# Rows of wo in one transfer per group, and loads of M's forms and stores of M at other places of a linear-attention kernel

## The chip, the cores and the metric

The kernel runs on one core of a Trainium2 chip. The time is the device time of one execution in microseconds; where several runs were made, their median. The profile is one further execution, recorded by the hardware profiler. Its span goes from the first to the last instruction.

## What is computed

Two linear-attention blocks, A and B, with the same shapes (x is 2048 x 640, 32 heads of 20), side by side in the output:

```python
qkv = (x @ wqkv).reshape(B, S, 3, H, Dh)             # q, k, v; H = 32, Dh = 20
phi = lambda t: jnp.where(t > 0, t + 1, jnp.exp(t)) + 1e-6
pq, pk = phi(q), phi(k)
kv = jnp.einsum("bhsd,bhse->bhde", pk, v)
z = jnp.einsum("bhsd->bhd", pk)
num = jnp.einsum("bhqd,bhde->bhqe", pq, kv)
den = jnp.einsum("bhqd,bhd->bhq", pq, z)[..., None] + 1e-6
return (num / den).transpose(...).reshape(B, S, D) @ wo     # of A and of B, concatenated
```

## The kernel before

**What it works on.** The values v are never formed. A Gram matrix G = phi(k)^T x is summed over the 2048 rows, each head's kv is G times its columns of wv, and M = kv times the rows of wo of that head: a 640 x 640 matrix per block. The output is then phi(q), divided by the denominators, times M. Products of fp32 values are split into a high and a low half (names ending in h and l) and made of three matmuls.

**Two phases.** In the first half (the k phase, to about 282 us) a planner orders the work. `note(engine, cost, function, writes, reads, ahead, dma, ...)` records a job with its cost and the transfer that it starts; the planner sorts the jobs of each engine by costs and due times. G of A and of B, and kv and M of A (`kvmm`, `mmm` L648), are made here. M of A goes to memory by SP (`md<-mev`, L670), and is read back (`m<-md`, L369) and turned into ten "forms" (sums and differences of blocks of M, split in two halves), which `m_forms` (L705) stores to memory (L713).

In the second half (the q phase) the order is written by hand: `at(slot, f, ...)` puts a call behind a slot, and the slots are `("q", u, c, k)`, unit u of 512 rows, chunk c of 5, step k of 5, and `("o", u, s)`. Units 0 to 3 are A's, 4 to 7 B's. `qmm` (L1144) makes q of a chunk: three matmuls per step (L1015 to L1017; in the first chunk of units 0 and 1, L1153, L1154 and, for the product with the low half of x, L1159 after the others). It needs x in two halves: `xqs`, loaded from the input and rounded by ScalarE (`load_xraw`, L1046), and `xql`, loaded from a copy that the k phase left in memory (`load_xq`, L1050). `psd` (L1193) are the denominators, `outmm` (L1289, matmuls L1313) the product with the forms. For A these are loaded by `form_load` (L1140: tiles `fh`, `fl`, `fm`, from `fdh`, `fdl`).

M of block B is made during unit 0 of the q phase: `load_o` loads the rows of wo, `kvmm2` makes kv, `mmm2` (called three times, i = 0 to 2, matmuls `psm` at L615) makes M of groups 2i and 2i + 1, and `store_m` stores it from GpSimd (L1082).

**The rows of wo.** The heads lie in six groups: four of 6 heads (120 rows of wo), two of 4 (80 rows). A tile of 128 partitions takes a group's first 64 rows in its lower half and the last 64 in its upper half; the halves share 8 or 48 rows, which the kv tile masks. `load_wo` (L628) loads it in two transfers of 64 rows on SP's queue, 160 KB each. In the k phase the planner calls it for A, two groups before each of three `mmm` (L653); in the q phase the slot ("q", 0, 0, 0) calls it for all six groups of B.

**Stores of M.** `m_rows` (L617) gives the rows of M of half a group: in memory 20 blocks of 3 (or 2) rows that lie 32 rows apart, in the tile 60 (or 40) partitions.

**Queues.** SP issues loads in its program order. Its transfers use eight semaphores in turn, so each is issued only when the one eight before it has landed.

Of the kernel before, what the change touches and what calls it, by code (L numbers as in the profile page):

```python
# [15 lines left out]
DH = 20  # L16
# [61 lines left out]
class Plan:  # L78
# [9 lines left out]
    def note(self, engine, n, fn, w, r, ahead=None, dma=None, late=None, by=None, due=None, safe=0.0, lat=0.0):  # L88
        base = self.RATE.get(engine)
        j = Job(engine, base[0] + base[1] * n if base else n, fn, ahead, dma)  # L90
        for part, writes in [(p, True) for p in w] + [(p, False) for p in r]:
            sp = part.space
            if sp.where is not None and sp not in j.spaces:
                j.spaces.append(sp)
            for lo, hi, other, wrote in sp.uses:
                if lo < part.hi and part.lo < hi and (writes or wrote) and other is not j:
                    j.deps.add(other)
            if writes:
                sp.uses = [u for u in sp.uses if not (part.lo <= u[0] and u[1] <= part.hi and u[2] is not j)]
            sp.uses.append((part.lo, part.hi, j, writes))  # L100
        for d in j.deps:
            d.nexts.append(j)
        for sp in j.spaces:
            sp.left += 1
        if engine == "PE":
            j.ideal = self.pe_at
            self.pe_at += j.cost
        j.late = self.pe_at + (25.0 if late is None else late)
        if by is not None:
            j.late = self.pe_at + by  # L110
        j.by, j.set, j.safe, j.lat = by, due, safe, (LAT if due is None else 1.9) + lat
        self.jobs.append(j)
        return j
# [105 lines left out]
def tile_linear_attn_pair(ctx: ExitStack, tc: tile.TileContext, ins, out: bass.AP):  # L219
    nc = tc.nc  # L220
    P = 128
    S, D = ins[0]["x"].shape
# [58 lines left out]
    note = plan.note  # L281
# [329 lines left out]
    def m_products(o, i, wo, hs):  # L611

        for p in (0, 64):
            for j in range(2):
                nc.tensor.matmul(o[p // 64][j * 64:j * 64 + 64, :HF],  # L615
                                 kvt[p:p + 64, 2 * i + j], wo[j][p:p + 64, hs], start=True, stop=True)

    def m_rows(b, i, a):

        rows = md[b].rearrange("(d h) n -> d h n", h=H)  # L620
        out = []
        for j in range(2):
            h0, nh = GROUPS[2 * i + j]
            n = nh // 2
            out.append((rows[:, h0 + a * n:h0 + a * n + n, :], slice(j * 64, j * 64 + DH * n)))
        return out

    def load_wo(eng, to, b, g):  # L628
        h0, nh = GROUPS[g]
        for p, row in ((0, h0 * DH), (64, (h0 + nh) * DH - 64)):  # L630
            eng.dma_start(to[p:p + 64], ins[b]["wo"][row:row + 64, :])

    def kvmm(k):
        ws = []
# [13 lines left out]
    def mmm(i):  # L648
        n = gn[0] - (3 if i % 2 else 4)
        ks = ((3, 4, 5)[n % 3], (3, 4, 5)[(n + 1) % 3], 6, 7)  # L650
        wo, m = ([Space(n, D, ANY) for _ in range(2)] for n in ("wo", "mev"))
        for j in range(2):
            note("SP", 0.14, lambda j=j: load_wo(nc.sync, wo[j].all.f, 0, 2 * i + j), [wo[j].all], [], ahead=14.0, dma=1.0)  # L653

        def products():
            for h in range(2):
                o = [BK[k].open("psm") for k in ks[2 * h:2 * h + 2]]
                m_products(o, i, [x.all.f for x in wo], slice(h * HF, h * HF + HF))

        note("PE", 1.3, products, [BK[k].all for k in ks], [x.all for x in wo] + [KVT.all])  # L660
        for h in range(2):
            hs = slice(h * HF, h * HF + HF)
            for a in range(2):
                k = ks[2 * h + a]
                note("ACT", HF, lambda a=a, k=k, hs=hs: act(m[a].all.f[:, hs], BK[k].tile[:, :HF], AF.Copy), [m[a][hs]],
                     [BK[k].all])
        for a in range(2):
            for j, (rows, part) in enumerate(m_rows(0, i, a)):
                w = 4 * i + 2 * a + j
                note("SP", 0.07, lambda a=a, rows=rows, part=part: nc.sync.dma_start(rows, m[a].all.f[part]),  # L670
                     [mdv[w:w + 1]], [m[a].all], dma=0.5)
# [87 lines left out]
    a, z, x = jh[0][0:P], jl[0][0:P], jr[0][0:P]  # L759
# [127 lines left out]
    for p in range(4, NPB):  # L887
        i, h = divmod(p - 2, 2)
# [9 lines left out]
    for p in range(NPB + 1, NP):  # L898
        if p == NPB + 1:
            fl = kvs  # L900
        else:
            i, h = divmod(p - NPB - 2, 2)
            gready(NG + i)
            fl = filled(NG + i, h, p in (NPB + 2, NP - 1))
        for (q, n), i in place.items():
            if q == p - NPB:
                fl.setdefault(n, []).append((mmm, i))
        kpair(p, fl)
        if p == NPB + 4:
            zsums(0)  # L910
        if p == NPB + 5:
            m_forms()
# [8 lines left out]
    j = note("HOST", 0.0, swap, [gate.all], [])  # L921
# [50 lines left out]
    for g, (h0, nh) in enumerate(GROUPS):  # L972
        cols = NC * DH * nh
        w = Space("wv", cols, (BD,))
# [46 lines left out]
    def at(slot, f, *a):  # L1021
        todo.setdefault(slot, []).append((f, a))
# [34 lines left out]
    def load_o(b, g):  # L1057
        tag = ("dsh0", "dsl0", "dsh1", "dsl1", "dah1", "dal1")[g]
        o = q2[0].tile([P, D], F32, name="wo", tag=tag, bufs=1)
        load_wo(nc.sync, o, b, g)  # L1060
        wot[b, g] = o
# [309 lines left out]
            at(a, form_split, b, i)  # L1371
            at(s, form_store, b, i)

    for i in range(6):
        at((("q", 0, 2, 1), ("q", 0, 2, 4), ("q", 0, 3, 1), ("q", 1, 0, 0), ("q", 1, 0, 2), ("q", 1, 1, 0))[i],
           form_load, 0, i)
    for i in range(6, 10):
        at(("q", 1, i - 5, 4) if i < 9 else ("q", 1, 4, 0), form_load, 0, i)

    for g in range(NGR):  # L1380
        at(("q", 0, 0, 0), load_o, 1, g)
# [1 line left out]
    for i in range(3):  # L1383
        at((("q", 0, 3, 1), ("q", 0, 4, 0), ("q", 0, 4, 4))[i], mmm2, 1, i)
        for h in range(2):
            at((("q", 0, 3, 3), ("q", 0, 3, 4), ("q", 0, 4, 2), ("q", 0, 4, 3), ("q", 1, 0, 1), ("q", 1, 0, 3))[2 * i + h],
               store_m, nc.gpsimd)

    for c, a in ((0, ("q", 1, 4, 1)), (2, ("q", 1, 4, 1)), (4, ("q", 2, 0, 3)), (1, ("q", 4, 0, 2)), (3, ("q", 4, 0, 2))):
# [11 lines left out]
    h = NG - 1  # L1401
# [26 lines left out]
    for v in range(1, NU):  # L1428
        w, u = v - 1, v + 1
# [8 lines left out]
        else:  # L1438
            a = (5, 6, 7, 8, 8, 10, 11) if v == 1 else (2, 3, 5, 6, 7, 9, 11)
# [75 lines left out]
```

## Time and profile before

| | |
|---|---|
| median of 3 runs | 567.69 us (566.89 to 568.5) |
| the profiled execution | 569.47 us |
| its span | 567.7 us, granted TensorE clock 0.994 |
| busy: PE, DVE, ACT, POOL | 557.9, 414.3, 351.5, 74.6 us |
| moved by the DMA engines | 119.60 MB, mean 211 GB/s |
| wo of A, wo of B | 12 and 12 transfers of 160 KB, 6.7 and 5.2 us to landing |

PE is TensorE's matmuls, PEld its weight loads, which overlap them; DVE is VectorE, ACT ScalarE, POOL GpSimd, SP the engine that only issues transfers. A row of the timeline has the start, the length, engine, line, operation and tiles, and in brackets the idle time ahead of it and what ended that. "SPq" and "POOL DMA_DIRECT2D" rows are issues of transfers: their length is that of the issuing, not of the transfer. "PEclk" is the granted clock as a share of the full one; the DMA share is the mean busy share of the core's 16 DMA engines (the packets' times add up to a little over 1 when all are full).

### The profile page before, as it was taken

What the parts mean: (1) busy time and instruction counts of PE and PEld (TensorE: products, weight loads), DVE (VectorE), ACT (ScalarE), POOL (GpSimd) and SP (SyncE); (2) the same over time, 40 slices, a digit from 0 to 9 for tenths busy, and PEclk for the clock granted to TensorE, in tenths of its full rate; (3) what the DMA queues carried; (4) which work ended last, traced back from release to release, by engine and by line L of the source; (5) the groups of instructions that cost most, each with busy time, mean ns of one, the idle gap of its engine ahead of it and who ended that gap; (6) DMA issues with size and microseconds to landing.
All of it is one profiled execution on the core that took longest, in us unless ns stands there. A gap on an engine that the chain in (4) does not pass through costs nothing.

```text
span 567.7 us, 9238 instructions
## 1 busy us (share of the span) xinstructions
PE 557.9 (98%) x3368; PEld 501.2 (88%) x3368; DVE 414.3 (73%) x657; ACT 351.5 (62%) x644; POOL 74.6 (13%) x127
## 2 busy tenths in 40 slices
PE   8999999999999999999999799999999999999997
PEld 6999999989998899998885589898989989898997
DVE  7788687589987668887632499967788686767792
ACT  6777475574768647676227268775767666665551
POOL 1210111111113001111215003110012201001010
PEclk9999999999999999999999799999999999999999
DMA  8994765849869577897999965763363997122022
GB/s 313 377 259 117 184 166 114 270 110 312 257 136 268 185 191 225 240 273 212 353 282 326 373 236 164 272 218 120 107 241 124 346 389 262 48 75 92 1 94 92
DMA packets 69509, 119.60 MB, mean 211 GB/s; under 512 B 7320, under 2 KB 30776, under 8 KB 69464
## 3 DMA queue, kind: packets, MB, share of 16 engines
q1 hardware_dynamic: 59576, 90.39, 48.0%
q0 software_dynamic: 9600, 28.23, 18.0%
q8 instruction: 26, 0.43, 0.3%
q10 hardware_dynamic: 288, 0.39, 0.3%
q14 instruction: 19, 0.16, 0.1%
HBM read 72.44 MB, written 36.07 MB: 191 GB/s over the span
## 4 chain that ended last, share of the span: by engine, by line
PE 93%; DMA 4%; DVE 2%; issue 0%; ACT 0%; SPq 0%; DVEq 0%; ACTq 0%
PE psg L547 19%; PE pa L1313 12%; PE ka L315 10%; PE psq L1015 7%; PE psq L1016 7%; PE psq L1017 7%; PE pe L1313 6%; PE ke L315 5%; PE psr L547 5%; PE psk L812 4%; PE psb L1313 4%; PE kb L315 3%; DMA xql<-xd 2%; PE pskv L602 1%; DMA xqs<-in_A_xt 1%; PE psm L615 1%
## 5 line engine op out<-in xcount | busy, mean ns | idle before, releaser
L1015 PE MATMUL psq<-xqh,wh 128*128 128x512 f32 x190 | 74.8, 394 | 0.0
L1017 PE MATMUL psq<-xqh,wl 128*128 128x512 f32 x190 | 74.6, 393 | 0.0
L1016 PE MATMUL psq<-xql,wh 128*128 128x512 f32 x190 | 74.5, 392 | 0.0
L547 PE MATMUL psg<-pkh,xnl 128*128 128x512 f32 x160 | 63.0, 394 | 0.0
L547 PE MATMUL psg<-pkl,xnh 128*128 128x512 f32 x160 | 63.0, 393 | 0.0
L547 PE MATMUL psg<-pkh,xnh 128*128 128x512 f32 x160 | 62.4, 390 | 0.0
L1173 DVE SCALAR_TENSOR_TENSOR pq<-eq,rq 128x512 f32<-128x512 f32 x40 | 27.6, 691 | 44.2 <-ACT rq L1172 44.2
L1171 ACT ACTIVATE eq<-psq 128x512 f32<-128x512 f32 x40 | 24.0, 600 | 55.3 <-PE psq L1017 44.7
L493 ACT ACTIVATE kt<-ka 128x320 f32<-128x320 f32 x52 | 22.6, 435 | 56.3 <-PE ka L315 56.1
L410 POOL DMA_DIRECT2D zacc<-ek x32 | 26.2, 819 | 198.2 <-DVE ek L503 164.8
L1328 ACT ACTIVATE o<-pa 128x320 f32<-128x320 f32 x64 | 27.9, 438 | 26.2 <-PE pa L1313 25.5
L1015 PEld LDWEIGHTS psq<-xqh,wh 128*128 128x128 f32 x190 | 36.0, 189 | 8.3 <-issue 1.0
L1017 PEld LDWEIGHTS psq<-xqh,wl 128*128 128x128 f32 x190 | 36.0, 189 | 7.7
L1016 PEld LDWEIGHTS psq<-xql,wh 128*128 128x128 f32 x190 | 36.0, 189 | 7.3
L547 PEld LDWEIGHTS psg<-pkh,xnl 128*128 128x128 f32 x160 | 30.0, 188 | 6.5
L547 PEld LDWEIGHTS psg<-pkh,xnh 128*128 128x128 f32 x160 | 30.1, 188 | 4.9
L547 PEld LDWEIGHTS psg<-pkl,xnh 128*128 128x128 f32 x160 | 30.0, 188 | 4.8
L503 DVE SCALAR_TENSOR_TENSOR ek<-ek,kt 128x640 f32<-128x640 f32 x26 | 21.4, 821 | 16.2 <-ACT kt L502 16.2
L405 ACT ACTIVATE pkh<-ek,epst 128x640 fp32r<-128x640 f32 x32 | 26.4, 827 | 5.7 <-DVE ek L503 5.7
L406 DVE SCALAR_TENSOR_TENSOR pkl<-ek,pkh 128x640 fp32r<-128x640 f32 x32 | 26.2, 820 | 3.7 <-ACT pkh L405 3.7
L560 DVE TENSOR_TENSOR gacc<-psg,gacc 128x512 f32<-128x512 f32 x30 | 20.5, 688 | 11.6 <-PE psg L547 11.3
L309 DVE TENSOR_TENSOR xnl<-xns,xnh 128x640 fp32r<-128x640 f32 x32 | 25.6, 819 | 0.8 <-ACT xnh L306 0.8
(225 smaller groups left out, 1638.4 us busy)
## 6 DMA issues: line engine op xcount, KB each, us to landing
zacc<-ek POOLq DMA_DIRECT2D x32, 320.0 KB, 4.6
xql<-xd SPq DMA_DIRECT2D x40, 256.0 KB, 5.7
xd<-xl SPq DMA_DIRECT2D x29, 320.0 KB, 4.0
out<-o POOLq DMA_DIRECT2D x28, 320.0 KB, 3.9
xns<-in_A_x SPq DMA_DIRECT2D x16, 320.0 KB, 4.6
xts<-in_B_xt_tiles SPq DMA_DIRECT2D x16, 320.0 KB, 4.4
xns<-in_B_x SPq DMA_DIRECT2D x16, 320.0 KB, 5.8
xqs<-in_A_xt SPq DMA_DIRECT2D x20, 256.0 KB, 6.2
```

What stands on the lines that cost most here:

```text
L309: note("DVE", n, lambda: tt(lo.r, src.f, hi.f, op=OP.subtract), [lo], [src, hi], ahead=10.0)
L315: nc.tensor.matmul(o, a.r, w.r, start=start and k == i == 0, stop=k == n - 1 and i == 2, skip_group_check=True)
L405: note("ACT", n + 110, lambda: act(hi.r, p.f, AF.Identity, bias=epst), [hi], [p, K0.all], by=8.0)
L406: note("DVE", n, lambda: stt(lo.r, p.f, EPS, hi.f, op0=OP.add, op1=OP.subtract), [lo], [p, hi], by=9.0)
L410: note("POOL", 1.0, lambda: nc.gpsimd.dma_start(z.f, p.f, **kw), [z], [p], dma=1.0 if first else 1.86)
L547: nc.tensor.matmul(o[:, :n], a.r, w.r, start=j == 0 and q == 0, stop=j == 2 and q == 2, skip_group_check=True)
L1015: nc.tensor.matmul(o, whi, xhi, start=first, stop=False)
L1016: nc.tensor.matmul(o, whi, xlo, start=False, stop=False)
L1017: nc.tensor.matmul(o, wlo, xhi, start=False, stop=last)
L1173: nc.vector.scalar_tensor_tensor(pq[u][:, c, :], e, 1.0, r, op0=OP.min, op1=OP.add)
L1313: nc.tensor.matmul(ps, x, y, start=start and n == i == 0, stop=n == len(terms) - 1 and i == 2, skip_group_check=True)
L1328: copy = lambda x, y: nc.scalar.activation(x, y, AF.Copy)
```

## The change

Three edits. `load_wo` makes one transfer of 128 rows in place of two of 64: the source is an access pattern of two runs of 64 rows that overlap, the second starting (20 nh - 64) rows after the first; the planner's cost of a call is halved. The loads of A's forms are called from other slots, with form 8 ahead of 6 and 7. The stores of B's M are called from later slots.

```diff
     def load_wo(eng, to, b, g):
         h0, nh = GROUPS[g]
-        for p, row in ((0, h0 * DH), (64, (h0 + nh) * DH - 64)):
-            eng.dma_start(to[p:p + 64], ins[b]["wo"][row:row + 64, :])
+        w = ins[b]["wo"][h0 * DH:(h0 + nh) * DH, :]
+        eng.dma_start(to, bass.AP(w.tensor, w.offset, [[(nh * DH - 64) * D, 2], [D, 64], [1, D]]))
...
-            note("SP", 0.14, lambda j=j: load_wo(nc.sync, wo[j].all.f, 0, 2 * i + j), [wo[j].all], [], ahead=14.0, dma=1.0)
+            note("SP", 0.07, lambda j=j: load_wo(nc.sync, wo[j].all.f, 0, 2 * i + j), [wo[j].all], [], ahead=14.0, dma=1.0)
...
-    for i in range(6):
-        at((("q", 0, 2, 1), ("q", 0, 2, 4), ("q", 0, 3, 1), ("q", 1, 0, 0), ("q", 1, 0, 2), ("q", 1, 1, 0))[i],
-           form_load, 0, i)
...
+    for i, a in ((0, ("q", 0, 1, 0)), (1, ("q", 0, 1, 3)), (2, ("q", 1, 0, 1)), (3, ("q", 1, 0, 4)), (4, ("q", 1, 1, 1)),
...
-            at((("q", 0, 3, 3), ("q", 0, 3, 4), ("q", 0, 4, 2), ("q", 0, 4, 3), ("q", 1, 0, 1), ("q", 1, 0, 3))[2 * i + h],
+            at((("q", 0, 4, 2), ("q", 0, 4, 3), ("q", 1, 0, 3), ("q", 1, 0, 4), ("q", 1, 1, 2), ("q", 1, 1, 3))[2 * i + h],
                store_m, nc.gpsimd)
```

The orders of TensorE, VectorE, ScalarE and GpSimd are the same in both programs, the stores of M on GpSimd included. SP's differs. This is SP at the start of the q phase in the kernel before (fdh_100 and fdl_101 are the halves of form 0, 102 and 103 of form 1, and so on; xd_87 is the copy of x of unit 1):

```order
L302 DMA wv<-in_B_wv 128x400 x2
L631 DMA wo<-in_B_wo 64x640 x12
L1046 DMA xqs<-in_A_xt 128x512
L1140 DMA fh<-fdh_100 128x640
L1140 DMA fl<-fdl_101 128x640
L1046 DMA xqs<-in_A_xt 128x512 x4
L1140 DMA fh<-fdh_102 128x640
L1140 DMA fl<-fdl_103 128x640
L1140 DMA fh<-fdh_104 128x640
L1140 DMA fl<-fdl_105 128x640
L1050 DMA xql<-xd_87 128x512 x5
```

And the same place of SP's order after the change:

```order
L302 DMA wv<-in_B_wv 128x400 x2
L631 DMA wo<-in_B_wo 128x1x640 x6
L1046 DMA xqs<-in_A_xt 128x512
L1140 DMA fh<-fdh_100 128x640
L1140 DMA fl<-fdl_101 128x640
L1140 DMA fh<-fdh_102 128x640
L1140 DMA fl<-fdl_103 128x640
L1046 DMA xqs<-in_A_xt 128x512 x4
L1050 DMA xql<-xd_87 128x512 x5
L1140 DMA fh<-fdh_104 128x640
L1140 DMA fl<-fdl_105 128x640
```

Twelve transfers of wo became six of 128 rows; form 1 moved ahead of four of the xqs, and form 2 behind the five xql of unit 1. In the k phase only the loads of wo differ; this is SP around the second of the three pairs of groups of A (xd_91 is the copy of x of unit 5, md_98 is M of A):

```order
 L349 DMA xd_91<-xl 640x1x128
 L302 DMA xts<-in_B_xt_tiles 128x640 x2
-L631 DMA wo<-in_A_wo 64x640 x4
+L631 DMA wo<-in_A_wo 128x1x640 x2
 L349 DMA xd_91<-xl 640x1x128 x2
 L670 DMA md_98<-mev 20x3x640 x4
```

Four transfers became two at the same place, ahead of the stores of x and of M.

More of the change, by code (lines that the diff above doesn't have):

```diff
@@ L1372, in forms2 @@
             at(s, form_store, b, i)
-    for i in range(6):
-        at((("q", 0, 2, 1), ("q", 0, 2, 4), ("q", 0, 3, 1), ("q", 1, 0, 0), ("q", 1, 0, 2), ("q", 1, 1, 0))[i],
-           form_load, 0, i)
-    for i in range(6, 10):
-        at(("q", 1, i - 5, 4) if i < 9 else ("q", 1, 4, 0), form_load, 0, i)
+    for i, a in ((0, ("q", 0, 1, 0)), (1, ("q", 0, 1, 3)), (2, ("q", 1, 0, 1)), (3, ("q", 1, 0, 4)), (4, ("q", 1, 1, 1)),
+                 (5, ("q", 1, 1, 4)), (8, ("q", 1, 2, 1)), (6, ("q", 1, 2, 4)), (7, ("q", 1, 3, 1)), (9, ("q", 1, 4, 0))):
+        at(a, form_load, 0, i)
     for g in range(NGR):
```

## The prediction

> **What bounds the kernel now.** I read the page first, then the waits of TensorE, then the chain, then the timeline round the one hole that the waits name.
>
> ```profile
> span 567.7 us, 9238 instructions
> PE 557.9 (98%) x3368; PEld 501.2 (88%) x3368; DVE 414.3 (73%) x657; ACT 351.5 (62%) x644; POOL 74.6 (13%) x127
> PE psq L1159 <- DMA xql<-xd: 4.4, 3, 3.5
> ```
>
> The first two lines are the page's, the third is from the waits of PE between 282 and 330 us (total, times, longest). TensorE is busy 98% of the span, and the one wait of a microsecond or more there is for the transfer xql. The chain (start, length, what) and TensorE's timeline show the place.
>
> ```profile
> 300.51 6.17 DMA xqs<-in_A_xt
> 306.75 10.28 DMA xql<-xd
> 317.07 1.93 PE psq L1159 x3
> ```
>
> ```profile
> 299.12 1.31 PE L615 MATMUL psm<-wo,kv 64*64 64x320 f32 x16
> 303.30 1.31 PE L615 MATMUL psm<-wo,kv 64*64 64x320 f32 x16
> 307.48 1.31 PE L615 MATMUL psm<-wo,kv 64*64 64x320 f32 x16
> ...
> 310.89 0.39 PE L1154 MATMUL psq<-xqh,wl 128*128 128x512 f32 x1
> 314.76 0.63 PE L1159 MATMUL psq<-xql,wh 128*128 128x512 f32 x1 [3.48 <-DMA xql<-xd]
> ...
> 321.79 0.41 PE L1194 MATMUL psd<-ac,same 128*128 128x512 f32 x1
> 322.04 0.40 PE L1015 MATMUL psq<-xqh,wh 128*128 128x512 f32 x1
> ```
>
> Three products M of block B (psm) run at 299.12, 303.30 and 307.48 without waiting. Then unit 1 runs dry at 311.1 and waits until xql has landed. From 310.89 to 322.04 only 14 matmuls start; at the step of 0.23 us of the others there (311.12 minus 310.89) they take 3.2 us, so the hole costs 11.15 - 3.2 = 7.9 us. Part of that is the clock, in the windows (span, then busy time of five engines, granted clock, DMA share, GB/s):
>
> ```profile
> 136.00:212.00 76.00, 76.00 (x570) 68.58 (x569) 57.26 (x103) 49.17 (x91) 12.85 (x18) 1.00 0.76 215
> 290.00:300.00 10.00, 9.73 (x156) 7.90 (x155) 2.98 (x6) 2.10 (x5) 2.19 (x4) 1.00 0.84 215
> 308.00:314.00 6.00, 3.28 (x22) 1.95 (x14) 2.01 (x3) 3.55 (x8) 2.38 (x4) 1.00 1.04 409
> 315.00:320.00 5.00, 4.11 (x8) 2.35 (x8) 0.00 (x0) 0.90 (x2) 0.00 (x0) 0.50 1.04 403
> ```
>
> After 3.5 us idle the granted clock is 0.50. The DMA engines are full from 308 to 320 (share 1.04, 409 GB/s), but between 290 and 300 they are 0.84 busy for 215 GB/s: that is where the twelve loads of wo, 64 rows each, are moving. So xql is late because transfers ahead of it on SP's queue move slowly.
>
> **The change, part by part.** TensorE's, VectorE's, ScalarE's and GpSimd's orders are the same in both programs; only SP's differs. The stores of M keep their place on GpSimd's queue, so that part does nothing it says: price zero. The form loads move behind other loads of SP. They are first read by outmm here:
>
> ```profile
> 334.31 0.32 PE L1313 MATMUL pa<-fh,dah 128*128 128x320 f32 x1
> ```
>
> That is 16 us behind the last xql (issued before 309.3), and the four form loads that stay in front keep this cover. Price zero while SP runs as now; if SP were late by more than 16 us with TensorE on time, they would cost the rest. Two form loads fewer stand ahead of xql: 2 x 0.33 MB / 409 GB/s = 1.6 us sooner for xql.
>
> What is left is load_wo: 18 transfers less to issue, and each of the 12 new ones reads two runs of 64 rows. How many DMA engines does such a transfer get? No load of this shape is in the trace, but the stores of M by SP tell something. A transfer ends with one packet of a few bytes on each engine that it used. These are windows of the DMA view, the first with an xd store alone (640 rows of 512 bytes), the second over the ends of four stores of M (60 rows each, 20x3 rows in memory):
>
> ```profile
> DMA packets 633, 0.33 MB, mean 133 GB/s; under 512 B 16, under 2 KB 632, under 8 KB 632
> ```
>
> ```profile
> 168.26 3.46 SPq L670 DMA_DIRECT2D md<-mev  x4
> ```
>
> ```profile
> DMA packets 322, 0.74 MB, mean 247 GB/s; under 512 B 40, under 2 KB 40, under 8 KB 320
> ```
>
> The first window (193.5 to 196 us) has 16 small packets, the second (171.2 to 174.2 us) 40: ten for each store of M. Sixty rows would divide into 15 engines of four rows. They went on ten, and ten is the largest number up to 16 that divides the 20 entries of the outermost count on the memory side, while 6 rows each come from the 60 on the other. So a transfer is cut between whole entries of an outermost count, never inside one. The new load of wo has 128 entries on the tile's side and **two** on the memory side, with 64 rows inside each. If whole entries count on both sides, it gets two engines. If only the destination counts, it gets 16; a cut into 16 would fall inside the source's entries. I take two.
>
> The Trainium skill, page "DMA: Bandwidth & Descriptors", section "Why a DMA increments its semaphore by 16 and not by 1", states it as a rule: the largest k up to 16 that divides the slowest dimension that is not 1 of both access patterns, on the lowest-numbered k engines. By that rule the stores of M get ten, as the trace has it, and the new load gets two, as in the sum below; it speaks against the reading by the destination alone, which this trace can't exclude.
>
> Price of one load: an engine moves 409 / (16 x 1.04) = 24.6 GB/s; a load of 128 rows of 2,560 bytes is 0.328 MB, half of it on each of two engines: 0.164 MB / 24.6 GB/s = 6.7 us, against 0.8 us on sixteen. All loads use the same two engines if these are fixed, so six are 40 us in a row; and since every other transfer of SP has a share on these engines, it ends only behind them.
>
> *q phase.* The issue rows:
>
> ```profile
> 285.54 11.21 SPq L631 DMA_DIRECT2D wo<-in_B_wo  x12
> ...
> 303.89 5.38 SPq L1050 DMA_DIRECT2D xql<-xd  x5
> ```
>
> The share falls below full at about 290, so I let the loads of wv before them end there. Two groups are in by 290 + 13.4 = 303.4, four by 316.8, six by 330.2, each with about 1 us to its semaphore (an estimate from the landing of xts, below). Products that run at 299.12, 303.30 and 307.48 then wait till 304.4, 317.8 and 331.2: stalls of 5.3, then 317.8 - (303.30 + 5.3) = 9.2, then 331.2 - (307.48 + 14.5) = 9.2: **23.7 us** in all. SP has eight transfers in flight (each waits for the one eight before it), so behind the last wo stand xqs, forms and xqs, then xql: about 3.9 MB, 9.4 us at 409 GB/s; xql's last lands at about 341 where it now lands at about 318, so the hole is kept and moves along with the rest, +23. Bounds: 22 (engines 5% quicker) and 27 (the half clock of the windows behind each stall, not all hidden in the next).
>
> *k phase.* Here the planner has the same order, with three pairs of wo loads; TensorE is never idle (76.00 of 76.00). Two engines now carry 0.76 x 76 = 58 us of work each between 136 and 212; without wo's 5 us (1.97 MB / 16 / 24.6 GB/s) and with six loads on two engines, 53 + 40 = 93 us in 76, so 17 us too much. What follows has this cover:
>
> ```profile
> 174.87 3.41 SPq L631 DMA_DIRECT2D wo<-in_A_wo  x4
> 188.71 1.14 SPq L302 DMA_DIRECT2D xts<-in_B_xt_tiles  x2
> ```
>
> ```profile
> xts<-in_B_xt_tiles SPq DMA_DIRECT2D x2, 320.0 KB, 3.2
> ```
>
> ```profile
> 200.85 0.72 ACT L306 ACTIVATE xh<-xts 128x640 fp32r<-128x640 f32 x1
> ```
>
> The two xts of 188.71 land 3.2 us later, the first at about 191.9, and are split at 200.85: 9 us of slack. 17 - 9 = 8 us of stall, and one or two returns from the half clock at up to 3.4 us (6.8 us at half speed): I take **13 us**. Bounds: 0 if the slack of all loads adds up; 33 if nearly all of 40 - 5 us comes through.
>
> Sum: 23.7 + 13 = 37 us. The profiled execution took 569.5 us (span 567.7), 1.8 above the median; on the median of 567.7 the sum gives **605 us**.
>
> **Rivals.**
>
> *Sixteen engines* (chance 0.10; the other side). The destination's 128 rows alone decide. Then wo moves at 409 instead of 215 GB/s: 1.97 MB in 4.8 us instead of 9.2, xql comes 4.4 + 1.6 = 6 us earlier, at 312, and the unit waits only for its own splits. For it: the window of 290 to 300 shows that 64-row loads are what is slow. Against it: a cut inside the source's entries, which no row shows. Up to 7.9 us, less about 1 for the sum and split behind it: 561 us. It decides as soon as a wo load's small packets count 16. The Trainium skill, page "SBUF — State Buffer", section "Door 1: The DMA port swizzle (why [64,N] ≈ [32,N])", says that partitions 0 to 63 reach only half of the ports, which agrees with the 215 GB/s and would give this gain; it says nothing of the number of engines.
>
> *Sixteen engines, and xql still late* (chance 0.05). SP's eight in flight and GpSimd's stores of M, which stay where they are, keep the engines full:
>
> ```profile
> 301.34 0.64 POOL L1082 DMA_DIRECT2D md<-mev  x1 [5.74 <-ACT mev L1076]
> ...
> 311.09 1.19 POOL L1082 DMA_DIRECT2D md<-mev  x2 [0.20 <-issue]
> ```
>
> Twelve stores (eight of 150 KB, four of 100 KB) are 1.6 MB or 4 us of all engines, just ahead of xql. Then half of the hole or more stays: 564 to 568 us, half of this within the 0.3% (1.7 us) that a measurement of this kernel can tell from no change.
>
> *Two engines, k phase covered.* The loads of x have more slack than the one that I read: 567.7 + 24 = 592. This is inside the forecast (two engines, 0.85), as is 628 with both upper bounds (567.7 + 27 + 33).
>
> **How the numbers follow.** Two engines: 0.85, all of it slower. Faster: 0.10 and 0.02 of the second rival, 0.12; within 0.3%: 0.03. The predicted time is 605. The range takes the forecast's bounds: 567.7 + 22 with nothing from the k phase, less 2 for the start at 290, is 588; the upper end is 628. It leaves out the two rivals and some of the tails, 2 in 10.
>
> **What would show it.** Right: in windows over the new wo loads, two small packets per load, a DMA share near 0.13 where only they move, 40 us from the first to the last landing; psm waiting for DMA wo three times in the q phase, 5 to 9 us each; waits in the k phase for splits of xts or xns; xql still waited for at about 340. Wrong: share near 1 at 400 GB/s after 290, sixteen small packets, and no wait at psm; then the time is near 561. If psm waits but the k phase has no idle time, only its 13 us were wrong.

## The result and the profile after

The changed kernel takes **609.42 us** (median of 4 runs, 608.88 to 610.76) against 567.93 us for the kernel before on the same chip: ratio 1.0735 (95% interval 1.0717 to 1.0753), 41.5 us more. Its profiled execution took 610.76 us, with a span of 609.0 us. Forecast was 605 us, 37 us more.

The page of the changed kernel (span, busy time, TensorE and its granted clock in 40 slices):

```profile
span 609.0 us, 9222 instructions
PE 565.8 (93%) x3368; PEld 506.4 (83%) x3368; DVE 414.0 (68%) x657; ACT 351.3 (58%) x644; POOL 74.5 (12%) x127
PE   8999999999898399999984379999999999999997
PEclk9999999999899599999996789999999999999999
```

Two dips have appeared, one around 200 us and a wider one from 316 to 365 us. The waits of TensorE over the whole span name them (total, times, longest):

```profile
PE ka L315 <- ACT kt L493: 13.1, 2, 11.4
PE psm L615 <- ACT mev L1076: 11.4, 1, 11.4
PE psm L615 <- DMA wo<-in_B_wo: 11.3, 3, 7.3
PE psq L1159 <- DMA xql<-xd: 1.2, 2, 0.7
```

Idle time is 13.1 + 11.4 + 11.3 + 1.2 and 0.7 for an xqh = 37.7 us, where the kernel before had 4.4 us (xql); waits of 1.0 us and less that both kernels have are left out. TensorE's busy time for the same 3368 matmuls is 7.9 us longer (565.8 against 557.9), which is the half clock behind the stalls. 33.3 + 7.9 = 41.2 us is the whole of the difference of the spans (41.3).

That the new load moves on two engines is plain in the windows. First a stretch in which only loads of wo move (DMA view, 316.5 to 322.5 us), then two stretches by windows (the last three columns are the granted clock, the DMA share and GB/s):

```profile
DMA packets 122, 0.31 MB, mean 51 GB/s; under 512 B 2, under 2 KB 2, under 8 KB 122
q1 hardware_dynamic: 122, 0.31, 12.9%
```

```profile
308.00:322.00 14.00, 10.71 (x156) 8.12 (x155) 3.44 (x6) 2.54 (x7) 2.19 (x4) 0.99 0.15 54
330.00:338.00 8.00, 3.00 (x16) 1.35 (x17) 0.00 (x0) 0.00 (x0) 0.00 (x0) 0.50 0.13 51
```

The first window holds nearly one load (0.31 of 0.328 MB) and two small packets, and 51 GB/s at a share of 0.13 is two of sixteen engines; at this rate one load takes 6.4 us. The pairs of small packets that end the first three loads come at 313.4, 319.9 and 326.3 us, also 6.4 us apart. Before the change the 64-row loads had run at 215 GB/s and a share of 0.84 in this place. SP's queue and the three products in the q phase now stand like this (timeline):

```profile
303.19 28.08 SPq L631 DMA_DIRECT2D wo<-in_B_wo  x6
331.38 6.18 SPq L1046 DMA_DIRECT2D xqs<-in_A_xt  x1
```

```profile
316.40 0.75 PE L615 MATMUL psm<-wo,kv 64*64 64x320 f32 x2
320.43 1.30 PE L615 MATMUL psm<-wo,kv 64*64 64x320 f32 x14 [3.29 <-DMA wo<-in_B_wo]
326.94 0.72 PE L615 MATMUL psm<-wo,kv 64*64 64x320 f32 x2 [0.73 <-DMA wo<-in_B_wo]
335.00 2.40 PE L615 MATMUL psm<-wo,kv 64*64 64x320 f32 x14 [7.33 <-DMA wo<-in_B_wo]
352.39 2.72 PE L615 MATMUL psm<-wo,kv 64*64 64x320 f32 x16 [11.41 <-ACT mev L1076]
```

```profile
350.41 0.63 ACT L1053 ACTIVATE xqh<-xqs 128x512 fp32r<-128x512 f32 x1 [27.77 <-DMA xqs<-in_A_xt]
351.90 1.42 ACT L1076 ACTIVATE mev<-psm 128x320 f32<-128x320 f32 x4
```

The first two products wait for wo itself. The third waits for ScalarE, which should have emptied the banks of the second product, but in its order the rounding of xqs (xqh, L1053) comes first; and xqs stands on SP's queue behind all six loads of wo. ScalarE was idle 27.8 us for it. In the k phase the same happens through the loads of x (chain, timelines of SP, of ScalarE and of TensorE):

```profile
180.86 25.16 DMA xns<-in_B_x x2
```

```profile
183.53 5.45 SPq L631 DMA_DIRECT2D wo<-in_A_wo  x2
189.08 6.42 SPq L302 DMA_DIRECT2D xns<-in_B_x  x2
```

```profile
206.05 0.74 ACT L306 ACTIVATE xnh<-xns 128x640 fp32r<-128x640 f32 x1 [13.71 <-DMA xns<-in_B_x]
```

```profile
207.16 0.63 PE L315 MATMUL ka<-wkh,xh 128*128 128x320 f32 x1 [11.37 <-ACT kt L493]
```

The 25.16 us of the chain are two loads of x, one after the other (x2). The first was issued at 180.86, ahead of the third pair of wo, and is rounded at 189.92. The second stands behind that pair: its issue starts at 189.08, and it is there at 206.0, 17 us later. ScalarE waits 13.7 us for it, with the emptying of TensorE's banks (kt) behind it in its order.

### The profile page after: what moved, and what is told of

Read it like the earlier page. It is cut to its first block, busy times and chain, and to the rows that moved or that the text cites. A ratio compares the mean times of both kernels' runs of the same rounds, so it can differ in the third digit from the quotient of the medians.

```text
span 609.0 us, 9222 instructions
## 1 busy us (share of the span) xinstructions
PE 565.8 (93%) x3368; PEld 506.4 (83%) x3368; DVE 414.0 (68%) x657; ACT 351.3 (58%) x644; POOL 74.5 (12%) x127
## 3 DMA queue, kind: packets, MB, share of 16 engines
q0 software_dynamic: 9600, 28.23, 16.9%
## 4 chain that ended last, share of the span: by engine, by line
PE 74%; DMA 16%; SPq 5%; DVE 2%; ACT 1%; issue 1%; ACTq 0%
PE psg L547 14%; PE pa L1313 11%; PE ka L315 8%; DMA xns<-in_B_x 7%; PE psq L1017 6%; PE psq L1016 6%; PE psq L1015 6%; PE pe L1313 5%; PE psk L812 4%; PE ke L315 4%; PE psr L547 3%; PE psb L1313 3%; SPq L631 3%; DMA xql<-xd 3%; DMA xqs<-in_A_xt 3%; DMA xd<-xl 3%
## 5 line engine op out<-in xcount | busy, mean ns | idle before, releaser
L1328 ACT ACTIVATE o<-pa 128x320 f32<-128x320 f32 x64 | 27.8, 437 | 26.3 <-PE pa L1313 26.0
L1053 ACT ACTIVATE xqh<-xqs 128x512 fp32r<-128x512 f32 x35 | 22.0, 629 | 29.3 <-DMA xqs<-in_A_xt 28.8
L315 PE MATMUL ka<-wkh,xh 128*128 128x320 f32 x78 | 25.1, 322 | 13.1 <-ACT kt L493 13.1
L306 ACT ACTIVATE xnh<-xns 128x640 fp32r<-128x640 f32 x32 | 22.4, 733 | 20.2 <-DMA xns<-in_B_x 20.2
L615 PE MATMUL psm<-wo,kv 64*64 64x320 f32 x96 | 11.8, 538 | 22.8 <-ACT mev L1076 11.4
```

The lines of the kernel that those rows point to most:

```text
L315: nc.tensor.matmul(o, a.r, w.r, start=start and k == i == 0, stop=k == n - 1 and i == 2, skip_group_check=True)
L1328: copy = lambda x, y: nc.scalar.activation(x, y, AF.Copy)
```

## The experiments

The theory is the forecast's: a transfer is cut only between entries of the outermost counts of both sides, so the new load gets two engines, and this is the whole loss. The rivals are that the moves of form loads take a part, that the rows read twice or the single transfer are what is slow, and that the loss would not split into the two phases. The times of the kernel before, each on the chip of the runs beside it, were 568.51 us in the first four runs, 568.15 in the second four and 568.39 in the last two.

**The new load alone**, in the old places:

```diff
-        for p, row in ((0, h0 * DH), (64, (h0 + nh) * DH - 64)):
-            eng.dma_start(to[p:p + 64], ins[b]["wo"][row:row + 64, :])
+        w = ins[b]["wo"][h0 * DH:(h0 + nh) * DH, :]
+        eng.dma_start(to, bass.AP(w.tensor, w.offset, [[(nh * DH - 64) * D, 2], [D, 64], [1, D]]))
```

> Only the new load_wo, with the form loads and the stores of M where they were. Theory (the load's two engines are the whole loss): 609 us as with the full change, within 2 us. Rival (the moves cost or give a part): over 3 us away from 609, towards 600 if the moves cost, towards 616 if they hid something.

Measured: 613.53 us, ratio 1.0796 (1.0782 to 1.0811). The load alone loses 45.0 us, 3.5 more than the whole change does (41.5): the rival is right in that the moves matter, but they give time back.

**The moves alone**, with the load as it was (the hunks on `form_load` and `store_m`, without those on `load_wo`):

> Only the moves of form loads and stores of M, wo still in two transfers of 64 rows. Theory: xql comes at most 1.6 us earlier (two form loads fewer ahead of it), 566 to 568 us; GpSimd's order is unchanged. Rival (the moves alone lose time): above 570 us.

Measured: 564.46 us, ratio 0.9938 (0.992 to 0.9956): 4.1 us faster, more than the 1.6 that I allowed. The window over the old hole (clock, share and GB/s last) and SP's issue of xql:

```profile
315.00:320.00 5.00, 5.00 (x24) 4.07 (x23) 4.17 (x4) 2.70 (x5) 0.00 (x0) 1.00 1.04 399
```

```profile
302.72 3.53 SPq L1050 DMA_DIRECT2D xql<-xd  x5
```

```profile
PE psq L1159 <- DMA xql<-xd: 1.0, 3, 0.6
```

The last xql is issued at about 306.3 instead of 309.3, the waits for it fall from 4.4 to 1.0 us, and the clock, which had been 0.50 here after a wait of 3.5 us, stays at 1.00. That is the profiled execution; over the six the mean granted clock lies between 0.994 and 1.000 and the time between 563.5 and 566.8 us, so the gain differs from one to the next. The stores of M stand in the same order on GpSimd's queue, so I put all of this down to the form loads; no run moves these alone.

**The new load in one phase only** (`if b == 1:` or `if b == 0:` ahead of the new lines, the old ones otherwise; the planner's cost stays as it was):

> The new load for block B in the q phase only. Theory: the q phase's loss as measured between the two profiles, 41.5 - 17.9 = 23.6 us, so 591 us, with waits at psm for wo and, through ScalarE, for xqs. Rival (the loss of the two phases is not additive, for instance the q phase's stalls come from the k phase's late transfers): under 584 us.

Measured: 597.13 us, ratio 1.0503 (1.0485 to 1.0521), 28.6 us more. That is 6 us above the 591 expected: the 23.6 us behind that number were the whole change's loss less 17.9, and so had the gain of the moves in them.

> The new load for block A in the k phase only. Theory: 17.9 us of loss in the k phase and nothing behind it, 585.6 us, with a wait of about 11 us near 210 us for a split of x. Rival (the planner's slack takes it up when the q phase is as before): under 575 us.

Measured: 585.37 us, ratio 1.0296 (1.0278 to 1.0314), 16.9 us more. The three parts add: 28.6 + 16.9 - 4.1 = 41.4 us, and the change as a whole measured 41.5. Neither phase's loss comes from the other. And 28.6 + 16.9 = 45.5 us is what the load alone lost in both phases (45.0) with the planner's cost halved, so the halved cost has no effect that these runs show. The waits of these two runs, q phase and then k phase:

```profile
PE psm L615 <- DMA wo<-in_B_wo: 12.3, 3, 7.3
PE psm L615 <- ACT mev L1080: 10.7, 1, 10.7
PE psq L1163 <- DMA xql<-xd: 3.6, 5, 1.0
```

```profile
PE ka L315 <- ACT kt L493: 12.6, 2, 10.0
PE psq L1163 <- DMA xql<-xd: 2.5, 2, 1.9
```

**How the source's count sets the engines.** In the next four runs wo is laid out in memory beforehand as the 128 rows of each group, so that no row is read twice; what differs is the outermost count of the source, which an unused row behind each block keeps at two or four. One transfer per group, form loads in the old places:

```diff
-        for p, row in ((0, h0 * DH), (64, (h0 + nh) * DH - 64)):
-            eng.dma_start(to[p:p + 64], ins[b]["wo"][row:row + 64, :])
+        eng.dma_start(to, ins[b]["wo"][g, :, :64])
...
-        "wo": np.ascontiguousarray(wo),
+        "wo": np.pad(np.stack([np.concatenate([wo[h0 * DH:h0 * DH + 64], wo[(h0 + nh) * DH - 64:(h0 + nh) * DH]])
+                              for h0, nh in GROUPS]).reshape(len(GROUPS), 2, 64, d), ((0, 0), (0, 0), (0, 1), (0, 0))),
```

> wo is laid out in memory beforehand as the 128 rows that a group's tile takes, in two blocks of 64 rows with an unused row behind each, so that the source keeps an outermost count of two, but no row is read twice; one transfer per group, places as before. Theory (outermost count of two gives two engines): as with the new load alone, 613.5 us within 2, two small packets per load. Rival (the shared rows are what is slow, or one transfer per group is): 561 to 570 us.

Measured: 614.43 us, ratio 1.0814 (1.0787 to 1.084). No row is read twice here, and the time is that of the new load alone (613.53). A window of 5.5 us over the loads (319 to 324.5):

```profile
DMA packets 112, 0.28 MB, mean 51 GB/s; under 512 B 2, under 2 KB 2, under 8 KB 112
```

> The same with four blocks of 32 rows. Theory: four engines, 3.3 us per load and 20 us for six; psm waits 1 to 3 us in place of 5 to 11 and xql comes about 10 us later than before the change: 575 to 583 us. Rival (the number of blocks doesn't matter): 613 us, or 568 us.

The edit is the same with `[g, :, :32]` and `reshape(len(GROUPS), 4, 32, d)`. Measured: 579.18 us, ratio 1.0193 (1.0169 to 1.0218). The window from 290 to 298, mostly loads of wo, and the waits:

```profile
290.00:298.00 8.00, 8.00 (x138) 6.99 (x137) 2.00 (x4) 1.30 (x3) 2.19 (x4) 1.00 0.33 111
```

```profile
PE psm L615 <- ACT mev L1075: 7.1, 1, 7.1
PE psq L1158 <- DMA xql<-xd: 2.8, 4, 1.2
PE psm L615 <- DMA wo<-in_B_wo: 1.1, 1, 1.1
```

111 GB/s, about twice the 51 of two engines. From 293 to 296.4 us, where SP's queue (q1) moves only loads of wo, it has a quarter of the sixteen engines; the small packets that end three of these loads come in fours (292.4 to 293.0, 295.6 to 296.3, 298.8 to 299.5 us).

```profile
q1 hardware_dynamic: 137, 0.34, 25.5%
```

The time is in the expected range, and so is the wait for wo, but the largest wait is again the one behind ScalarE, which the expectation didn't count.

> The same with all 128 rows of a group in one block (outermost count 128 on both sides), places as before. Theory: sixteen engines at the full rate, six groups in 5 us where the 64-row loads take 9; xql about 4 us sooner, so 3 to 7 us off the hole: 561 to 565 us. Rival (64-row loads were not the limit ahead of xql): 567 to 569 us.

```diff
+        eng.dma_start(to, ins[b]["wo"][g])
```

Here the rows lie without gaps, 128 entries on both sides. Measured: 561.6 us, ratio 0.9886 (0.9867 to 0.9905). The waits name no transfer any more, and SP has issued the six loads in 5 us:

```profile
285.20 5.01 SPq L630 DMA_DIRECT2D wo<-in_B_wo  x6
```

```profile
284.00:290.00 6.00, 6.00 (x28) 4.95 (x28) 2.67 (x4) 2.15 (x4) 0.57 (x1) 1.00 1.01 369
```

> One block per group and the moves of the form loads as in the change: the change as it would be with sixteen engines. Theory: the hole of 7.9 us is closed once only, so no sum of the two gains: 560 to 563 us, no wait for xql. Rival (the moves' gain is of another kind than the hole and adds): 557 to 559 us.

The same two lines put into the changed kernel. Measured: 561.92 us, ratio 0.9889 (0.9872 to 0.9906). The moves add nothing to the 561.6 us before them: they and the wider load close the same hole. So 561.6 us, with the old places, is the best time here, 1.1% below the kernel before. The laying out of wo is done before the kernel starts and is in none of these times.

**The loads of block B from GpSimd's queue.** One line (`load_o` calls `load_wo(nc.gpsimd, o, b, g)`), first with the new load in the q phase, then with the old one:

> The new load for block B only (as in the run that changed the q phase alone, 597.1 us), but issued from GpSimd's queue, so that SP's queue holds no load of wo in the q phase. Theory (most of the q phase's loss is the row of six loads on one pair of engines; what SP's own blocked issue adds is the third stall, of 10.7 us behind ScalarE): if GpSimd's loads use one pair too, psm still waits for wo, 15 to 20 us in all, and 583 to 592 us; the stall behind ScalarE is gone. Rival (GpSimd's loads go to different pairs, so they move side by side): no wait for wo, 560 to 568 us.

Measured: 579.08 us, ratio 1.0187 (1.0162 to 1.0212), between the two theories. The issue of the six loads on GpSimd, their size and median time to landing, a window over them and the wait:

```profile
295.03 4.82 POOL L632 DMA_DIRECT2D wo<-in_B_wo  x6 [0.42 <-issue]
```

```profile
wo<-in_B_wo POOLq DMA_DIRECT2D x6, 320.0 KB, 17.4
```

```profile
300.00:306.00 6.00, 0.00 (x0) 0.00 (x0) 0.04 (x1) 0.00 (x0) 0.00 (x0) 0.81 1.20 220
```

```profile
PE psm L615 <- DMA wo<-in_B_wo: 14.3, 1, 14.3
```

The one wait of 14.3 us is for the first product only: the six loads were issued from 295.0 to 299.9 and landed between 313.0 and 315.9. So here they do move side by side, as the rival said: in a row on one pair they would land 6.4 us apart. But each is under way for 17.4 us, and GpSimd issues them 9.5 us later than SP did (285.5), behind its own transfers of z. The number of 560 to 568 us was therefore wrong too. The DMA view of the same window shows what fills the engines (q0 is GpSimd's queue):

```profile
DMA packets 2032, 1.32 MB, mean 220 GB/s; under 512 B 1578, under 2 KB 1578, under 8 KB 2032
q0 software_dynamic: 1605, 0.42, 63.1%
```

GpSimd's queue takes 0.63 of the share of 1.20 and moves 0.42 of the 1.32 MB; the rest are SP's loads. Most of its packets are under 512 bytes. Whether these are why each load takes 17.4 us this run doesn't settle. The run doesn't separate SP's blocked issue from the shares either, since both changed.

> The kernel before, with the twelve 64-row loads of block B issued from GpSimd's queue. SP is then free of them and can issue xqs and xql up to 10 us sooner. Theory (what made xql late is SP's order and eight in flight behind the slow 64-row loads): hole mostly gone, 561 to 565 us. Rival (the 64-row loads slow the engines whoever issues them, and all the rest moves at the same time): 566 to 569 us.

Measured: 571.2 us, ratio 1.0043 (1.0029 to 1.0057). Slower by less than 1%, and slower than either theory. The wait for xql is gone, as the theory has it, but psm now waits for wo:

```profile
PE psm L615 <- DMA wo<-in_B_wo: 4.8, 2, 3.1
```

The hole has only moved from the transfers behind wo to wo.

## Why the prediction was right, and where its steps were off

- *Two engines for the new load*: right, and shown. Two small packets per load, 51 GB/s, share 0.13; two blocks without shared rows cost the same, four blocks a quarter as much (11.0 us), one block nothing. The reading by the destination alone is excluded, since the destination was 128 rows in all of them.
- *6.7 us per load*: 6.4 measured. *A stall of 5.3, then twice 9.2 us at psm, 23.7 in all*: 4.0, 7.3 and 11.4, together 22.8 us. That the total comes so near is in part luck: the third has another path than the one I named, not wo but ScalarE's rounding of xqs ahead of the emptying of a bank. I had seen that xqs stands behind wo on SP's queue, but not who waits for it.
- *The hole at xql is kept*: wrong in the changed kernel, 1.2 us against 4.4. Most of this is the moves of the form loads: with them alone 1.0 us is left, with the new load alone 2.7, and with it in the q phase alone 3.6.
- *q phase 23.7 us, at most 27*: 28.6 measured, above the bound. The step that failed is the clock, which I had hidden in the next stall. In the run with the new load in the q phase alone, idle time rose by 26.6 - 4.4 = 22.2 us and TensorE's busy time by 563.1 - 557.9 = 5.2 us, together 27.4 (the spans of the two profiled executions differ by 27.1).

```profile
PE 563.1 (95%) x3368; PEld 503.6 (85%) x3368; DVE 414.2 (70%) x657; ACT 350.7 (59%) x644; POOL 74.6 (13%) x127
```

- *k phase 13 us*: 16.9 measured. The half clock was near (5.1 us of busy time; I had 5), the stall was 12.6 instead of 8: I took the slack of xts, 9 us, for what follows the loads, and the first to be late was xns, which has far less. In the kernel before, the two xns behind the third pair of wo land 7.8 to 8.3 us after the start of their issue (178.37 and 179.90) and are rounded from 188.68 and 189.84 on, about 2 us after landing. 17 - 2 would have been 15 us, so the 17 us were also somewhat too many. SP and ScalarE of the kernel before, then the page of the run with the new load in the k phase alone:

```profile
178.37 2.33 SPq L302 DMA_DIRECT2D xns<-in_B_x  x2
188.68 0.73 ACT L306 ACTIVATE xnh<-xns 128x640 fp32r<-128x640 f32 x1
```

```profile
PE 563.0 (96%) x3368; PEld 505.6 (87%) x3368; DVE 414.4 (71%) x657; ACT 350.9 (60%) x644; POOL 74.4 (13%) x127
```

- *The moves of the form loads, price zero*: wrong by 4.1 us. I worked out that xql would come sooner, and counted nothing for it, because I kept the hole as it was. Two form loads fewer in front made xql earlier by 3 us and, with it, took away the half clock. *The stores of M, price zero*: nothing in GpSimd's order moved, and no run shows an effect.
- Together: 4.9 + 3.9 - 4.1 = 4.7 us, which is what the forecast's 36.7 us lacks of 41.5, to 0.1. The two phases were 8.8 us short and the moves made up for 4.1 of it, so that 605 lies within 5 us of 609.4 is in part luck. The direction and the two engines behind it were not luck.
- *Sixteen engines, 561 us*, the rival: the state it assumed never came about in the change, but its number was right for it: one block measured 561.6 and 561.9 us.

The Trainium skill's rule (page "DMA: Bandwidth & Descriptors", section "Why a DMA increments its semaphore by 16 and not by 1") agrees with every count seen here on SP's queue: 16, 10, 4 and 2 small packets. By the Trainium skill, page "SBUF — State Buffer", section "Door 1: The DMA port swizzle (why [64,N] ≈ [32,N])", partitions 0 to 63 reach half of the ports, and 64 to 127 the other half. The 215 GB/s of the 64-row loads against 369 GB/s in the window with the one-block loads agree with that; no run here shows the ports themselves.

## What to carry to other kernels

Before two transfers are put into one, look at the outermost count of the new one on both sides: a source in two pieces put a load on two of the sixteen engines, and half as many transfers cost 45 us. Look then at who stands behind it on the queue, since everything issued later has its share on the same engines; the dearest stall of TensorE in the q phase (11.4 us) came through ScalarE, which reads none of these loads. And where the layout can be chosen, lay the rows out so that one run covers all partitions: that made the gain of a single transfer real, 561.6 us.

## What was not expected of the hardware

- **SP's issue itself blocks.** From the third load of wo on, each issue on SP lasts about as long as a load (5.1, 6.3, 6.3 and 8.0 us): six take 28.08 us, the xqs behind them 6.18 us, where an issue of wo took 0.47 to 0.68 us in this place before. With four blocks six take 10.62 us, with one block 5.01. So a queue of transfers on few engines also stops the issuing of transfers that would use the others. What this costs beside the shares was not separated. An estimate: the small packets that end the fourth load come at 334.5 us, two more loads of 6.4 us end at about 347, and the first xqs is there at 350.4; its shares behind the loads would alone have kept it until about then.
- **The same loads from GpSimd's queue move side by side**: six issued within 5 us, each 17.4 us under way, all landing within 3 us. The DMA share of 1.20 there is no sign of speed: 0.63 of it is GpSimd's queue, which moves 0.42 MB in 6 us (70 GB/s).
- **The clock**: in the changed kernel every wait of TensorE from 1.75 us on (1.75, 11.4, 3.3, 7.3 and 11.4 us) was followed by matmuls at a granted clock of 0.50. Waits that stayed under 1 us (the moves alone) left it at 1.00, but behind five waits for xql of at most 1.0 us in a row (the new load in the q phase alone) it was 0.50 from 345.8 to 349 us. In the changed kernel this is 7.9 of the 41.2 us. The kernel before pays too: with one block per group, at a mean clock of 0.999, TensorE is busy for 554.9 us, so by an estimate the half clock takes 3.0 us of the kernel before and 10.9 us of the changed one.
